# Gated linear attention into a two-layer MLP: attention output produced already transposed, with a reordered start and one more bank at the end

## The chip, the cores and the metric

The kernel runs on one core of a Trainium2 chip. The core has five engines that each run their own queue of instructions in order: TensorE (PE; matmuls, with weight loads listed as PEld), VectorE (DVE), ScalarE (ACT), GpSimd (POOL) and SyncE (SP, which here only issues DMAs). They meet through semaphores. Data lies in SBUF (128 partitions); matmuls write PSUM, which has eight banks. The metric is the device time of one execution in microseconds; the time of the kernel before is the median of 3 runs.

## The reference

The inputs q, k, v and f_logit are each (4, 8, 768, 48): batch B, heads H, time S, head dimension D. In float32:

```
f = 1 / (1 + exp(-f_logit))
for t in range(S):
    state = f[:, :, t, :, None] * state + einsum('bhd,bhde', k_t, v_t)
    y[:, :, t] = einsum('bhd,bhde->bhe', q_t, state)
x = y.transpose(0, 2, 1, 3).reshape(3072, 384)
h = x @ w_in            # 384 x 2048
out = maximum(0.01 * h, h) @ w_out   # 2048 x 384
```

The output is (3072, 384) float32.

## The kernel before

**Units.** Time is cut into chunks of 128 steps. A unit is one chunk of one batch entry with all 8 heads: 6 chunks x 4 batch entries = 24 units, numbered chunk by chunk, so that units 0 to 3 are the first chunk of each batch entry (c == 0) and units 20 to 23 the last. A state per batch entry is carried from chunk to chunk, in float32 (state_f) and bf16 (state_b); heads lie in pairs, two to a block of 128 columns, each head padded from 48 to 64.

**Attention of a unit.**
- load (L82): four DMAs on SP, f, k, q, v, 192 KB each, into pool inp with 6 buffers per name.
- gate_act (L106): ScalarE computes exp and log of f; gate_pe (L113): TensorE sums the logs over time with a triangular matrix ut, and the whole chunk's sum per column.
- decay_act (L124): ScalarE turns the sums into two factors, em and a, and the chunk's decay a_end.
- scale (L137): kh = k * em and qh = q * a. For units 0 and 1 kh is on VectorE; all else is on GpSimd.
- cast_v (L143): GpSimd copies v to bf16.
- turn_pe, turn_dve (L149, L156): TensorE transposes kh and qh in pairs of heads into one PSUM bank (ps_t); VectorE copies kT out, and copies q out in two 64-partition halves into qbd, a block-diagonal form whose other blocks are zero (cleared once, L75).
- score_pe (L165): four matmuls of kT against 256 columns of qbd; each gives the scores of two heads. Two banks (ps_w), each filled by two matmuls. mask_dve (L175): VectorE multiplies each bank by ut.
- mix_pe (L182): y, with time in the partitions and heads in the columns. For c > 0 eight matmuls of qbd with state_b (48 columns each), then eight of the masked scores with v (48 columns each).
- state_pe, state_dve, state_pool (L200, L211, L220): the new state, with the float32 update on VectorE and GpSimd and one bf16 copy on GpSimd. The last chunk skips these.
- y_act, x_pe, x_dve (L228, L233, L240): ScalarE copies y to bf16, TensorE transposes it in three blocks of 128 columns, VectorE copies the result out as xT, with the model dimension in the partitions.

**MLP of a unit.** up (L246) is called in four quarters: 12 matmuls of w_in against xT into one of two banks (ps_m), then a leaky ReLU on ScalarE into g. down (L258) is called in two halves of eight matmuls each (384 columns), which accumulate in the one bank of ps_o (pm2); the first half reads the first half of w_out, the second half the second. put (L265): VectorE copies pm2 to osb, SP writes it out.

**Weights.** load_w_in (L91) is called twice, each time for half of the 2048 columns and with three DMAs on the queue of GpSimd; load_w_out (L97) is called twice with one DMA each. They convert from float32 to bf16 on the way. GpSimd issues them in its own order: it works through what stands ahead of them first.

**Order.** Nothing is reordered: each engine runs its instructions as the program writes them. First come the loads of units 0 to 4 (LA = 5), then a start written out by hand (L278 to L324): attention of unit 0 with the w_in loads, gates of unit 1, the first two quarters of up of unit 0, the first w_out half, the other two quarters, then attention of unit 1 with the gates of unit 2 in it. The loop (L326) goes over i = 1 to 25: load unit i + 4; turn unit i + 1; half of up of unit i; scores and masks of i + 1; gate, decay and scale of i + 2; the other half of up; mix and state of i + 1; gate_act of i + 3; half of down of unit i - 2 (LAG = 2); the turn of x of i + 1; the other half of down, and put. PSUM is full: 2 banks for up, 1 for down, 1 for the turns, 2 for scores, 2 shared (ps_s, tag sm) by the gate sums, y, the new state and the turned x.

Of the kernel before, what the change touches and what calls it, by code (L numbers as in the profile page):

```python
# [9 lines left out]
FP32 = mybir.dt.float32  # L10
# [5 lines left out]
def kernel(  # L16
# [22 lines left out]
    NU = len(units)  # L39

    const = ctx.enter_context(tc.tile_pool(name="const", bufs=1))
    inp = ctx.enter_context(tc.tile_pool(name="inp", bufs=6))
    work = ctx.enter_context(tc.tile_pool(name="work", bufs=3))
    gpool = ctx.enter_context(tc.tile_pool(name="gpool", bufs=5))
    opool = ctx.enter_context(tc.tile_pool(name="opool", bufs=4))
# [22 lines left out]
    lfs = [const.tile([128, H, 64], BF16, name=f"lf{i}", tag=f"lf{i}") for i in range(3)]  # L68
    qhs = [const.tile([128, H, 64], BF16, name=f"qh{i}", tag=f"qh{i}") for i in range(3)]
    khs = [const.tile([128, H, 64], BF16, name=f"kh{i}", tag=f"kh{i}") for i in range(3)]  # L70
    qbds = [const.tile([128, P2, 2, 128], BF16, name=f"qbd{i}", tag=f"qbd{i}") for i in range(2)]
    state_f = [const.tile([128, P2, D], FP32, name=f"sf{b}", tag=f"sf{b}") for b in range(B)]
    state_b = [const.tile([128, P2, D], BF16, name=f"sb{b}", tag=f"sb{b}") for b in range(B)]
    for t in lfs + qhs + khs + qbds:
        nc.vector.memset(t, 0.0)  # L75
    for t in state_f:
        nc.vector.memset(t, 0.0)


    raw = {}  # L80

    def load(u):  # L82
        c, b = units[u]
        r = {}
        for name, src in (("f", f_logit), ("k", k), ("q", q), ("v", v)):
            t = inp.tile([128, H, D], FP32, name=f"{name}_raw", tag=f"{name}_raw")
            nc.sync.dma_start(out=t, in_=src[b, :, c * C:(c + 1) * C, :].rearrange("h t d -> t h d"))
            r[name] = t
        raw[u] = r

    def load_w_in(part, parts):  # L91
        w = FF // parts
        for kk in range(NK):
            nc.gpsimd.dma_start(out=w_in_b[:, kk, part * w:(part + 1) * w],  # L94
                                in_=moe_w_in[kk * 128:(kk + 1) * 128, part * w:(part + 1) * w])
# [7 lines left out]
    st = {}  # L103


    def gate_act(u):  # L106
        f = raw[u]["f"]
        e = work.tile([128, H, D], FP32, name="e_t", tag="e_t")
        nc.scalar.activation(e, f, AF.Exp, scale=-1.0)  # L109
        lf = lfs[u % 3]  # L110
        nc.scalar.activation(lf[:, :, 0:D], e, AF.Ln, bias=1.0)  # L111
# [31 lines left out]
    def cast_v(u):  # L143
        r = raw.pop(u)
        v_b = work.tile([128, H, D], BF16, name="v_b", tag="v_b")
        nc.gpsimd.tensor_copy(out=v_b, in_=r["v"])  # L146
        st[u]["v"] = v_b

    def turn_pe(u):  # L149
        tp = ps_t.tile([128, 2, P2, 128], BF16, name="tp", tag="tp")  # L150
        for i, src in enumerate((khs[u % 3], qhs[u % 3])):
            for p in range(P2):
                nc.tensor.transpose(tp[:, i, p, :], src[:, 2 * p:2 * p + 2, :], ident)  # L153
        st[u]["tp"] = tp

    def turn_dve(u):  # L156
        tp = st[u].pop("tp")
        kT = work.tile([128, P2, 128], BF16, name="kT", tag="kT")
        nc.vector.tensor_copy(out=kT, in_=tp[:, 0])  # L159
        qbd = qbds[u % 2]  # L160
        nc.vector.tensor_copy(out=qbd[0:64, :, 0, :], in_=tp[0:64, 1])
        nc.vector.tensor_copy(out=qbd[64:128, :, 1, :], in_=tp[64:128, 1])  # L162
        st[u]["kT"] = kT

    def score_pe(u):  # L165
        kT, qbd = st[u].pop("kT"), qbds[u % 2]
        st[u]["pw"] = []
        for g in range(2):
            pw = ps_w.tile([128, 4, 128], FP32, name="pw", tag="pw")
            for i in range(2):  # L170
                p = 2 * g + i
                nc.tensor.matmul(pw[:, 2 * i:2 * i + 2, :], kT[:, p, :], qbd[:, p, :, :], start=True, stop=True)  # L172
            st[u]["pw"].append(pw)

    def mask_dve(u):  # L175
        st[u]["wm"] = []
        for pw in st[u].pop("pw"):
            wm = work.tile([128, 4, 128], BF16, name="wm", tag="wm", bufs=6)
            nc.vector.tensor_mul(wm, pw, ut[:, None, :].to_broadcast([128, 4, 128]))  # L179
            st[u]["wm"].append(wm)  # L180

    def mix_pe(u):  # L182
        c, b = units[u]
        s = st[u]
        qbd, v_b, wms = qbds[u % 2], s["v"], s.pop("wm")
        py = ps_s.tile([128, 512], FP32, name="py", tag="sm")
        n = H if c == 0 else 2 * H
        i = 0
        if c > 0:
            for h in range(H):  # L190
                nc.tensor.matmul(py[:, h * D:(h + 1) * D], qbd[:, h // 2, h % 2, :], state_b[b][:, h // 2, :],  # L191
                                 start=(i == 0), stop=(i == n - 1))
                i += 1
        for h in range(H):
            nc.tensor.matmul(py[:, h * D:(h + 1) * D], wms[h // 4][:, h % 4, :], v_b[:, h, :],  # L195
                             start=(i == 0), stop=(i == n - 1))
            i += 1
        s["py"] = py

    def state_pe(u):  # L200
        c, b = units[u]
        if c == NCH - 1:
            return
        kh, v_b = khs[u % 3], st[u]["v"]
        pt = ps_s.tile([128, P2, 2 * D], FP32, name="pt", tag="sm")
        for p in range(P2):
            nc.tensor.matmul(pt[:, p, :], kh[:, 2 * p:2 * p + 2, :], v_b[:, 2 * p:2 * p + 2, :],  # L207
                             start=True, stop=True)
        st[u]["pt"] = pt
# [10 lines left out]
    def state_pool(u):  # L220
        c, b = units[u]
        if c == NCH - 1:
            return
        sf = state_f[b]
        nc.gpsimd.tensor_mul(sf, sf, st[u]["a_end"][:, :, None].to_broadcast([128, P2, D]))  # L225
        nc.gpsimd.tensor_copy(out=state_b[b], in_=sf)

    def y_act(u):  # L228
        xn = work.tile([128, KD], BF16, name="xn", tag="xn")
        nc.scalar.copy(out=xn, in_=st[u].pop("py")[:, 0:KD])  # L230
        st[u]["xn"] = xn

    def x_pe(u):  # L233
        xn = st[u].pop("xn")
        px = ps_s.tile([128, NK, 128], BF16, name="px", tag="sm")
        for kk in range(NK):
            nc.tensor.transpose(px[:, kk, :], xn[:, kk * 128:(kk + 1) * 128], ident)  # L237
        st[u]["px"] = px

    def x_dve(u):  # L240
        xT = work.tile([128, NK, 128], BF16, name="xT", tag="xT", bufs=6)
        nc.vector.tensor_copy(out=xT, in_=st[u].pop("px"))  # L242
        st[u]["xT"] = xT


# [12 lines left out]
    def down(u, half):  # L258
        s = st[u]
        if half == 0:  # L260
            s["pm2"] = ps_o.tile([128, KD], FP32, name="pm2", tag="pm2")
        for ff in range(8 * half, 8 * half + 8):
            nc.tensor.matmul(s["pm2"], s["g"][:, ff, :], w_out_b[:, ff, :], start=(ff == 0), stop=(ff == NF - 1))  # L263

# [5 lines left out]
        st.pop(u)  # L270


    LA = 5
    LAG = 2
    for u in range(LA):
        load(u)

    gate_act(0)  # L278
    gate_pe(0)
    decay_act(0)  # L280
    scale(0)
    load_w_in(0, 2)
    cast_v(0)
    load_w_in(1, 2)
    turn_pe(0)
    turn_dve(0)
    score_pe(0)
    mask_dve(0)
    mix_pe(0)
    y_act(0)  # L290
    x_pe(0)
    x_dve(0)
    state_pe(0)
    state_dve(0)
    state_pool(0)

    gate_act(1)
    gate_pe(1)
    decay_act(1)
    up(0, 0)  # L300
    up(0, 1)
    scale(1)
    cast_v(1)
    load_w_out(0, 2)
    up(0, 2)
    up(0, 3)
    turn_pe(1)
    turn_dve(1)
    gate_act(2)
    gate_pe(2)  # L310
    score_pe(1)
    mask_dve(1)
    decay_act(2)
    scale(2)
    cast_v(2)
    load_w_out(1, 2)
    mix_pe(1)
    y_act(1)
    x_pe(1)
    x_dve(1)  # L320
    state_pe(1)
    state_dve(1)
    state_pool(1)
    gate_act(3)  # L324

    for i in range(1, NU + LAG):  # L326
        n1, n2, n3, d = i + 1, i + 2, i + 3, i - LAG
        if i + LA - 1 < NU:
            load(i + LA - 1)
        if n1 < NU:  # L330
            turn_pe(n1)
            turn_dve(n1)
        if i < NU:
            up(i, 0)
            up(i, 1)
        if n1 < NU:
            score_pe(n1)
            mask_dve(n1)
        if n2 < NU:
            gate_pe(n2)  # L340
            decay_act(n2)
            scale(n2)
            cast_v(n2)
        if i < NU:
            up(i, 2)
            up(i, 3)
        if n1 < NU:
            mix_pe(n1)
            y_act(n1)
            state_pe(n1)  # L350
            state_dve(n1)
            state_pool(n1)
        if n3 < NU:
            gate_act(n3)
        if d >= 0:
            down(d, 0)
        if n1 < NU:
            x_pe(n1)
            x_dve(n1)
        if d >= 0:  # L360
            down(d, 1)
            put(d)

# [29 lines left out]
```

## Time and profile before

| | |
|---|---|
| median of 3 runs | 205.89 us (205.06 to 206.22) |
| the profiled execution | 205.08 us, of it a span of 203.3 us from first to last instruction |
| TensorE busy | 183.2 us, 90% of the span |
| ScalarE, VectorE, GpSimd busy | 109.2, 98.6, 75.3 us |
| share of TensorE in the chain that ended last | 85% (L254 up 32%, L263 down 31%) |
| share of DMA in that chain | 7% |
| moved by DMA | 25.17 MB read, 4.72 MB written |

How to read the lines below. A page line of an engine has its busy time, share of the span and count; the rows of digits give, for 40 equal slices of the span, the busy share in tenths. A line of the chain has start, length, engine, tile and line of the kernel. A timeline line has start, length, engine, line, operation, what is written <- what is read, shapes, count, and in brackets the idle time before it with what ended it. Matmuls are pipelined, so the recorded length of a group is longer than the distance from its start to the next group's start. q0 is the DMA queue that GpSimd issues to, q1 that of SP.

### The profile page before, as it was taken

What the parts mean: (1) busy time and instruction counts of PE and PEld (TensorE: products, weight loads), DVE (VectorE), ACT (ScalarE), POOL (GpSimd) and SP (SyncE); (2) the same over time, 40 slices, a digit from 0 to 9 for tenths busy, and PEclk for the clock granted to TensorE, in tenths of its full rate; (3) what the DMA queues carried; (4) which work ended last, traced back from release to release, by engine and by line L of the source; (5) the groups of instructions that cost most, each with busy time, mean ns of one, the idle gap of its engine ahead of it and who ended that gap; (6) DMA issues with size and microseconds to landing.
All of it is one profiled execution on the core that took longest, in us unless ns stands there. A gap on an engine that the chain in (4) does not pass through costs nothing.

```text
span 203.3 us, 5831 instructions
## 1 busy us (share of the span) xinstructions
PE 183.2 (90%) x2432; PEld 149.2 (73%) x2432; DVE 98.6 (48%) x225; ACT 109.2 (54%) x237; POOL 75.3 (37%) x127
## 2 busy tenths in 40 slices
PE   0446778999999999999999999999999999999973
PEld 0224658977887887897788788789779878877741
DVE  8450155654664565455465456445546534533021
ACT  4142446856844854764674584485467458533400
POOL 2743064536415514623641651562363244120000
PEclk9999999999999999999999999999999999999999
DMA  6999999999976946865874785595585671110111
GB/s 132 189 158 203 191 200 179 186 191 201 215 144 116 193 95 128 172 136 106 152 165 97 128 173 116 109 194 126 111 155 118 141 135 42 40 41 2 42 54 62
DMA packets 106267, 27.12 MB, mean 133 GB/s; under 512 B 100352, under 2 KB 105472, under 8 KB 106240
## 3 DMA queue, kind: packets, MB, share of 16 engines
q1 hardware_dynamic: 103296, 23.60, 59.7%
q0 software_dynamic: 2944, 3.15, 9.4%
q8 instruction: 19, 0.31, 0.7%
q14 instruction: 8, 0.07, 0.1%
HBM read 25.17 MB, written 4.72 MB: 147 GB/s over the span
## 4 chain that ended last, share of the span: by engine, by line
PE 85%; DMA 7%; ACT 3%; POOL 2%; DVE 1%; issue 1%
PE pm L254 32%; PE pm L263 31%; PE pw L172 6%; DMA w_in_b<-in_moe_w_in_dram 5%; PE tp L153 5%; PE py L195 2%; PE px L237 2%; PE cs L117 2%; PE py L191 2%; PE pt L207 2%; DMA f_raw<-in_f_logit_dram 1%; POOL w_in_b L94 1%; DVE osb L268 1%; PE cs L120 1%; DVE wm L179 1%
## 5 line engine op out<-in xcount | busy, mean ns | idle before, releaser
L256 ACT ACTIVATE gT<-pm 128x512 bf16<-128x512 f32 x96 | 56.2, 601 | 63.0 <-PE pm L254 61.3
L254 PE MATMUL pm<-xT,w_in_b 128*128 128x128 bf16 x1152 | 76.0, 224 | 3.9 <-DMA w_in_b<-in_moe_w_in_dram 3.9
L254 PEld LDWEIGHTS <-w_in_b 128*128 128x128 bf16 x1152 | 69.2, 101 | 5.4 <-DMA w_in_b<-in_moe_w_in_dram 4.7
L263 PE MATMUL pm<-w_out_b,gT 128*128 128x384 bf16 x384 | 69.7, 326 | 1.3 <-DVE osb L268 1.3
L140 POOL TENSOR_TENSOR kh<-k_raw,em_t 128x384 bf16<-128x384 f32 x22 | 20.1, 915 | 93.0 <-ACT em_t L129 88.2
L263 PEld LDWEIGHTS <-gT 128*128 128x128 bf16 x384 | 35.4, 98 | 20.9 <-issue 1.8
L179 DVE TENSOR_TENSOR wm<-pw,ut 128x512 bf16<-128x512 f32 x48 | 30.9, 687 | 12.6 <-PE pw L172 12.6
L268 DVE COPY osb<-pm 128x384 f32<-128x384 f32 x24 | 13.4, 558 | 30.4 <-PE pm L263 30.4
L141 POOL TENSOR_TENSOR qh<-q_raw,a_t 128x384 bf16<-128x384 f32 x24 | 21.9, 914 | 4.6 <-ACT a_end L133 4.5
L242 DVE COPY xT<-px 128x384 bf16<-128x384 bf16 x24 | 8.6, 358 | 23.6 <-PE px L237 23.6
L217 DVE TENSOR_TENSOR sf<-sf,pt 64x192 f32<-64x192 f32 x20 | 6.9, 346 | 20.9 <-PE pt L207 19.3
L172 PE MATMUL pw<-qbd,kT 128*128 128x256 bf16 x96 | 15.2, 282 | 1.3 <-DVE qbd L162 1.3
L159 DVE COPY kT<-tp 128x512 bf16<-128x512 bf16 x24 | 10.0, 417 | 11.2 <-PE tp L153 11.0
L109 ACT ACTIVATE e_t<-f_raw 128x384 f32<-128x384 f32 x24 | 12.8, 533 | 4.8 <-DMA f_raw<-in_f_logit_dram 4.8
L129 ACT ACTIVATE em_t<-cs 128x384 bf16<-128x384 f32 x24 | 11.8, 491 | 6.1 <-PE cs L120 5.2
L230 ACT CAST xn<-py 128x384 bf16<-128x384 f32 x24 | 11.4, 473 | 6.6 <-PE py L195 6.6
L117 PE MATMUL cs<-lf,ut 128*128 128x384 bf16 x24 | 8.3, 345 | 5.8 <-ACT lf L111 5.8
L111 ACT ACTIVATE lf<-e_t 128x384 bf16<-128x384 f32 x24 | 12.6, 523 | 0.8
L172 PEld LDWEIGHTS <-kT 128*128 128x128 bf16 x96 | 9.4, 99 | 4.2 <-DVE kT L159 0.8
L146 POOL CAST v_b<-v_raw 128x384 bf16<-128x384 f32 x24 | 12.1, 504 | 0.6 <-DMA v_raw<-in_v_dram 0.6
L130 ACT ACTIVATE a_t<-cs 128x384 bf16<-128x384 f32 x24 | 11.6, 484 | 0.0
L225 POOL TENSOR_TENSOR sf<-sf,a_end 128x192 f32<-128x192 f32 x20 | 10.1, 505 | 3.7 <-DVE sf L218 3.7
(38 smaller groups left out, 153.5 us busy)
## 6 DMA issues: line engine op xcount, KB each, us to landing
f_raw<-in_f_logit_dram SPq DMA_DIRECT2D x24, 192.0 KB, 3.1
k_raw<-in_k_dram SPq DMA_DIRECT2D x24, 192.0 KB, 4.4
q_raw<-in_q_dram SPq DMA_DIRECT2D x24, 192.0 KB, 4.2
v_raw<-in_v_dram SPq DMA_DIRECT2D x24, 192.0 KB, 4.3
out_dram<-osb SPq DMA_DIRECT2D x24, 192.0 KB, 2.0
w_in_b<-in_moe_w_in_dram POOLq DMA_DIRECT2D x6, 256.0 KB, 8.4
w_out_b<-in_moe_w_out_dram POOLq DMA_DIRECT2D x2, 768.0 KB, 9.7
```

The costliest lines, as they stand in the source:

```text
L109: nc.scalar.activation(e, f, AF.Exp, scale=-1.0)
L111: nc.scalar.activation(lf[:, :, 0:D], e, AF.Ln, bias=1.0)
L117: nc.tensor.matmul(cs[:, 0:H * D], ut, lf[:, :, 0:D], start=True, stop=True)
L140: eng.tensor_mul(khs[u % 3][:, :, 0:D], r["k"], st[u]["em"])
L141: nc.gpsimd.tensor_mul(qhs[u % 3][:, :, 0:D], r["q"], st[u]["a"])
L146: nc.gpsimd.tensor_copy(out=v_b, in_=r["v"])
L172: nc.tensor.matmul(pw[:, 2 * i:2 * i + 2, :], kT[:, p, :], qbd[:, p, :, :], start=True, stop=True)
L179: nc.vector.tensor_mul(wm, pw, ut[:, None, :].to_broadcast([128, 4, 128]))
L254: nc.tensor.matmul(pm[:, i, :], w_in_b[:, kk, ff * 128:(ff + 1) * 128], s["xT"][:, kk, :], start=(kk == 0), stop=(kk == NK - 1))
L256: nc.scalar.activation(s["g"][:, 4 * g:4 * g + 4, :], pm, AF.Prelu, alpha=0.01)
L263: nc.tensor.matmul(s["pm2"], s["g"][:, ff, :], w_out_b[:, ff, :], start=(ff == 0), stop=(ff == NF - 1))
L268: nc.vector.tensor_copy(out=osb, in_=st[u]["pm2"])
```

## The change

- **x comes out transposed.** mix_pe now writes y with the model dimension in the partitions, straight into a tile py of [128, 3, 128], and y_act, x_pe and x_dve give way to one VectorE copy from PSUM, y_dve. The 384 rows of the result are cut into 12 groups of 32; group g lies in block g // 4 at partitions 32 * (g % 4). A pair of heads has three groups: 32 columns of the first head, 16 of each, 32 of the second. For c > 0 each group takes one matmul with 32 columns of state_b as weights and the pair's qT (128 columns) as moving data. For the masked scores each pair takes four: the outer groups from v_b, and the middle group twice from v2, a copy of v's middle 32 columns spread to 64 with 16 zero columns beside each half.
- **Scores without the block-diagonal q.** turn_dve copies q out whole as qT. score_pe takes eight matmuls of 48 partitions and 128 columns, one per head, the first heads of the pairs into one bank and the second heads into the other, alternating.
- **What this brings along.** qbd goes; v2 (three tiles, cleared once, filled by GpSimd in cast_v) comes. state_b becomes block-diagonal, twice as wide, cleared once, and GpSimd fills it by two copies of 64 partitions.
- **The start.** Only units 0 and 1 are loaded at first. A DMA of two elements on SP, hold, reads from the third piece of w_in's first half, so SP waits until that piece has landed; then it issues unit 2, and units 3 to 5 behind it. The pool inp has 7 buffers. The order of units 0 to 2 is new: half of up of unit 0, attention of unit 1, half of up of unit 1, gates of unit 2, w_out, the rest of up of unit 0, and attention of unit 2 with the rest of up of unit 1 and the gates of unit 3 between its parts. The loop begins at i = 2.
- **Two last banks.** The last even unit's down (unit 22) accumulates in the bank of the turns, not in that of ps_o.

```diff
-    inp = ctx.enter_context(tc.tile_pool(name="inp", bufs=6))
+    inp = ctx.enter_context(tc.tile_pool(name="inp", bufs=7))
...
-    qbds = [const.tile([128, P2, 2, 128], BF16, name=f"qbd{i}", tag=f"qbd{i}") for i in range(2)]
+    v2s = [const.tile([128, P2, 4, 16], BF16, name=f"v2{i}", tag=f"v2{i}") for i in range(3)]
...
-    state_b = [const.tile([128, P2, D], BF16, name=f"sb{b}", tag=f"sb{b}") for b in range(B)]
-    for t in lfs + qhs + khs + qbds:
+    state_b = [const.tile([128, P2, 2 * D], BF16, name=f"sb{b}", tag=f"sb{b}") for b in range(B)]
+    for t in lfs + qhs + khs + v2s + state_b:
         nc.vector.memset(t, 0.0)
...
+    hold = const.tile([1, 2], BF16, tag="hold")
...
+        v2 = v2s[u % 3]
+        nc.gpsimd.tensor_copy(
+            out=v2[:, :, 0:4:3, :],
+            in_=r["v"].rearrange("t (p j) d -> t p (j d)", j=2)[:, :, 32:64].rearrange("t p (j e) -> t p j e", j=2))
...
-        qbd = qbds[u % 2]
-        nc.vector.tensor_copy(out=qbd[0:64, :, 0, :], in_=tp[0:64, 1])
-        nc.vector.tensor_copy(out=qbd[64:128, :, 1, :], in_=tp[64:128, 1])
+        qT = work.tile([128, P2, 128], BF16, name="qT", tag="qT")
+        nc.vector.tensor_copy(out=qT, in_=tp[:, 1])
...
-        for g in range(2):
-            pw = ps_w.tile([128, 4, 128], FP32, name="pw", tag="pw")
-            for i in range(2):
-                p = 2 * g + i
-                nc.tensor.matmul(pw[:, 2 * i:2 * i + 2, :], kT[:, p, :], qbd[:, p, :, :], start=True, stop=True)
+        pws = [ps_w.tile([128, P2, 128], FP32, name="pw", tag="pw") for j in range(2)]
+        for p in range(P2):
+            for j in range(2):
+                rows = slice(64 * j, 64 * j + D)
+                nc.tensor.matmul(pws[j][:, p, :], kT[rows, p, :], qT[rows, p, :], start=True, stop=True)
...
+    NQ = 3 * P2
...
+        py = ps_s.tile([128, NK, 128], FP32, name="py", tag="sm")
+        jobs = []
         if c > 0:
+            for g in range(NQ):
+                p, i = divmod(g, 3)
+                jobs.append((g, state_b[b][:, p, 32 * i:32 * i + 32], qT[:, p, :]))
+        for j in range(2):
+            for p in range(P2):
+                jobs.append((3 * p + 2 * j, v_b[:, 2 * p + j, 16 * j:16 * j + 32], wms[j][:, p, :]))
+            for p in range(P2):
+                jobs.append((3 * p + 1, v2[:, p, 2 * j:2 * j + 2, :], wms[j][:, p, :]))
+        left = [sum(1 for g, _, _ in jobs if g % 4 == r) for r in range(4)]
+        begun = [False] * 4
+        for g, lhsT, rhs in jobs:
+            kk, r = divmod(g, 4)
+            left[r] -= 1
+            nc.tensor.matmul(py[32 * r:32 * r + 32, kk, :], lhsT, rhs, start=not begun[r], stop=left[r] == 0)
+            begun[r] = True
...
-        nc.gpsimd.tensor_copy(out=state_b[b], in_=sf)
+        for j in range(2):
+            rows = slice(64 * j, 64 * j + 64)
+            nc.gpsimd.tensor_copy(out=state_b[b][rows, :, j * D:j * D + D], in_=sf[rows])
-    def y_act(u):
...
-    def x_pe(u):
...
-    def x_dve(u):
+    def y_dve(u):
         xT = work.tile([128, NK, 128], BF16, name="xT", tag="xT", bufs=6)
-        nc.vector.tensor_copy(out=xT, in_=st[u].pop("px"))
+        nc.vector.tensor_copy(out=xT, in_=st[u].pop("py"))
...
-            s["pm2"] = ps_o.tile([128, KD], FP32, name="pm2", tag="pm2")
+            pool, tag = (ps_t, "tp") if u >= NU - 2 and u % 2 == 0 else (ps_o, "pm2")
+            s["pm2"] = pool.tile([128, KD], FP32, name="pm2", tag=tag)
```

The start and the loop after the change; attend(u) is turn, scores, masks, mix, y_dve and state of one unit, one after another:

```
    LA = 4
    load(0)
    load(1)
    gate_act(0)
    gate_pe(0)
    decay_act(0)
    scale(0)
    load_w_in(0, 2)
    nc.sync.dma_start(out=hold, in_=w_in_b[0:1, NK - 1, 0:2])
    cast_v(0)
    load_w_in(1, 2)
    load(2)
    attend(0)
    gate_act(1)
    gate_pe(1)
    decay_act(1)
    scale(1)
    cast_v(1)
    up(0, 0)
    up(0, 1)
    attend(1)
    up(1, 0)
    up(1, 1)
    gate_act(2)
    gate_pe(2)
    decay_act(2)
    scale(2)
    load_w_out(0, 2)
    cast_v(2)
    load_w_out(1, 2)
    load(3)
    load(4)
    load(5)
    up(0, 2)
    up(0, 3)
    turn_pe(2)
    turn_dve(2)
    up(1, 2)
    score_pe(2)
    mask_dve(2)
    gate_act(3)
    gate_pe(3)
    decay_act(3)
    scale(3)
    cast_v(3)
    up(1, 3)
    mix_pe(2)
    y_dve(2)
    state_pe(2)
    state_dve(2)
    state_pool(2)
    gate_act(4)

    for i in range(2, NU + LAG):
...
        if n1 < NU:
            mix_pe(n1)
            y_dve(n1)
...
        if d >= 0:
            down(d, 0)
            down(d, 1)
            put(d)
```

More of the change, by code (lines that the diff above doesn't have):

```diff
@@ L146, in cast_v @@
         nc.gpsimd.tensor_copy(out=v_b, in_=r["v"])
-        st[u]["v"] = v_b
+        v2 = v2s[u % 3]
+        nc.gpsimd.tensor_copy(
+            out=v2[:, :, 0:4:3, :],
+            in_=r["v"].rearrange("t (p j) d -> t p (j d)", j=2)[:, :, 32:64].rearrange("t p (j e) -> t p j e", j=2))
+        st[u]["v"], st[u]["v2"] = v_b, v2
     def turn_pe(u):
@@ L159, in turn_dve @@
         nc.vector.tensor_copy(out=kT, in_=tp[:, 0])
-        qbd = qbds[u % 2]
-        nc.vector.tensor_copy(out=qbd[0:64, :, 0, :], in_=tp[0:64, 1])
-        nc.vector.tensor_copy(out=qbd[64:128, :, 1, :], in_=tp[64:128, 1])
-        st[u]["kT"] = kT
+        qT = work.tile([128, P2, 128], BF16, name="qT", tag="qT")
+        nc.vector.tensor_copy(out=qT, in_=tp[:, 1])
+        st[u]["kT"], st[u]["qT"] = kT, qT
     def score_pe(u):
-        kT, qbd = st[u].pop("kT"), qbds[u % 2]
-        st[u]["pw"] = []
-        for g in range(2):
-            pw = ps_w.tile([128, 4, 128], FP32, name="pw", tag="pw")
-            for i in range(2):
-                p = 2 * g + i
-                nc.tensor.matmul(pw[:, 2 * i:2 * i + 2, :], kT[:, p, :], qbd[:, p, :, :], start=True, stop=True)
-            st[u]["pw"].append(pw)
+        kT, qT = st[u].pop("kT"), st[u]["qT"]
+        pws = [ps_w.tile([128, P2, 128], FP32, name="pw", tag="pw") for j in range(2)]
[3 more added lines that the diff above has]
+                nc.tensor.matmul(pws[j][:, p, :], kT[rows, p, :], qT[rows, p, :], start=True, stop=True)
+        st[u]["pw"] = pws
     def mask_dve(u):
@@ L177, in mask_dve @@
         for pw in st[u].pop("pw"):
-            wm = work.tile([128, 4, 128], BF16, name="wm", tag="wm", bufs=6)
-            nc.vector.tensor_mul(wm, pw, ut[:, None, :].to_broadcast([128, 4, 128]))
+            wm = work.tile([128, P2, 128], BF16, name="wm", tag="wm", bufs=6)
+            nc.vector.tensor_mul(wm, pw, ut[:, None, :].to_broadcast([128, P2, 128]))
             st[u]["wm"].append(wm)
+    NQ = 3 * P2
     def mix_pe(u):
@@ L184, in mix_pe @@
         s = st[u]
[L185 to L188, printed above, removed]
+        qT, v_b, v2, wms = s.pop("qT"), s["v"], s.pop("v2"), s.pop("wm")
+        py = ps_s.tile([128, NK, 128], FP32, name="py", tag="sm")
+        jobs = []
         if c > 0:
[L190 to L197, printed above, removed]
+            for g in range(NQ):
[13 more added lines that the diff above has]
+            begun[r] = True
         s["py"] = py
@@ L225, in state_pool @@
         nc.gpsimd.tensor_mul(sf, sf, st[u]["a_end"][:, :, None].to_broadcast([128, P2, D]))
-        nc.gpsimd.tensor_copy(out=state_b[b], in_=sf)
-    def y_act(u):
-        xn = work.tile([128, KD], BF16, name="xn", tag="xn")
-        nc.scalar.copy(out=xn, in_=st[u].pop("py")[:, 0:KD])
-        st[u]["xn"] = xn
-    def x_pe(u):
[L234 to L238, printed above, removed]
-    def x_dve(u):
+        for j in range(2):
+            rows = slice(64 * j, 64 * j + 64)
+            nc.gpsimd.tensor_copy(out=state_b[b][rows, :, j * D:j * D + D], in_=sf[rows])
+    def y_dve(u):
         xT = work.tile([128, NK, 128], BF16, name="xT", tag="xT", bufs=6)
-        nc.vector.tensor_copy(out=xT, in_=st[u].pop("px"))
+        nc.vector.tensor_copy(out=xT, in_=st[u].pop("py"))
         st[u]["xT"] = xT
@@ L270, in put, with attend @@
         st.pop(u)
-    LA = 5
+    LA = 4
     LAG = 2
-    for u in range(LA):
-        load(u)
+    def attend(u):
+        turn_pe(u)
+        turn_dve(u)
+        score_pe(u)
+        mask_dve(u)
+        mix_pe(u)
+        y_dve(u)
+        state_pe(u)
+        state_dve(u)
+        state_pool(u)
+    load(0)
+    load(1)
     gate_act(0)
@@ L282 @@
     load_w_in(0, 2)
+    nc.sync.dma_start(out=hold, in_=w_in_b[0:1, NK - 1, 0:2])
     cast_v(0)
     load_w_in(1, 2)
[L285 to L295, printed above, removed]
+    load(2)
+    attend(0)
     gate_act(1)
@@ L299 @@
     decay_act(1)
+    scale(1)
+    cast_v(1)
     up(0, 0)
     up(0, 1)
-    scale(1)
-    cast_v(1)
-    load_w_out(0, 2)
+    attend(1)
+    up(1, 0)
+    up(1, 1)
+    gate_act(2)
+    gate_pe(2)
+    decay_act(2)
+    scale(2)
+    load_w_out(0, 2)
+    cast_v(2)
+    load_w_out(1, 2)
+    load(3)
+    load(4)
+    load(5)
     up(0, 2)
     up(0, 3)
[L307 to L323, printed above, removed]
-    gate_act(3)
-    for i in range(1, NU + LAG):
+    turn_pe(2)
[3 more added lines that the diff above has]
+    mask_dve(2)
+    gate_act(3)
+    gate_pe(3)
[10 more added lines that the diff above has]
+    for i in range(2, NU + LAG):
         n1, n2, n3, d = i + 1, i + 2, i + 3, i - LAG
-        if i + LA - 1 < NU:
-            load(i + LA - 1)
+        if i + LA < NU:
+            load(i + LA)
         if n1 < NU:
@@ L348 @@
             mix_pe(n1)
-            y_act(n1)
+            y_dve(n1)
             state_pe(n1)
@@ L356 @@
             down(d, 0)
[L357 to L360, printed above, removed]
             down(d, 1)
```

## The prediction

> **What bounds the kernel now.** I read the page's busy rows first, then the chain that ended last, then the timeline of one iteration, then the start and the end. From the page:
>
> ```profile
> PE 183.2 (90%) x2432; PEld 149.2 (73%) x2432; DVE 98.6 (48%) x225; ACT 109.2 (54%) x237; POOL 75.3 (37%) x127
> PE   0446778999999999999999999999999999999973
> DMA  6999999999976946865874785595585671110111
> ```
>
> TensorE is full from the eighth slice (about 36 us) on; before that it has holes while the DMA engines are full. So there are two regimes, a start of some 36 us and a dense loop, and a short tail. One iteration in the chain (start, us, what):
>
> ```profile
> 94.09 0.45 PE tp L153 x8
> 94.54 1.34 PE pm L254 x24
> 95.88 0.57 PE pw L172 x4
> 96.69 1.36 PE pm L254 x24
> 98.25 0.20 PE py L195 x8
> 98.63 1.30 PE pm L263 x8
> 100.09 1.30 PE pm L263 x8
> 101.39 0.45 PE tp L153 x8
> ```
>
> It is TensorE alone, 101.39 - 94.09 = 7.30 us per unit: no other engine appears. The timeline of the same iteration gives the pieces to be replaced:
>
> ```profile
> 95.38 0.43 DVE L162 COPY qbd<-tp 64x512 bf16<-64x512 bf16 x1
> 95.86 0.60 PE L172 MATMUL pw<-qbd,kT 128*128 128x256 bf16 x4
> 97.89 0.36 PE L191 MATMUL py<-sb,qbd 128*128 128x48 bf16 x8
> 98.09 0.36 PE L195 MATMUL py<-v_b,wm 128*128 128x48 bf16 x8
> 98.30 0.33 PE L207 MATMUL pt<-v_b,kh 128*128 128x96 bf16 x4
> ```
>
> Recorded lengths contain a latency, so I go from start to start. Up's first half starts at 94.38 and takes 24 x 56 ns, to 95.72; the scores start at 95.86, when the third VectorE copy ends: a stall of 0.14. Scores 0.43 (95.86 to 96.29, when the gate starts). Mix 97.89 to 98.30 = 0.41, or 16 pairs of weight load and matmul at 25.6 ns each. The three turns of x (L237) start at 99.76, the next layer's half at 99.93: 0.17. Together 0.14 + 0.43 + 0.41 + 0.17 = 1.15 us of the 7.30. A 128-column matmul is 56 ns, a 384-column one 162.5 ns (1.30 / 8).
>
> **The loop after the change.** Out go the stall (two copies of about 0.4 us instead of three end 0.4 us earlier), four 256-column scores, sixteen mix matmuls and three turns. In come eight scores of 128 columns on 48 rows each, and in mix 12 matmuls from the state and 16 from the masks, each with 32 weight columns and 128 moving columns. The trace has no matmul on a part of the array. Bounds: serial at 56 ns, 36 x 56 = 2.02 us. From below, two scores abreast and four mix matmuls abreast, 4 x 56 + 7 x 56 = 0.62 us. Between stands the pair rate of the old mix, the fastest that any weight load with matmul goes in this trace: 36 x 25.6 = 0.92 us. I take it, since it is the row nearest in kind (many small matmuls, each with its own weights). Then an iteration changes by 0.92 - 1.15 = -0.23 us; with 20 full iterations (units 4 to 23 attended in the loop) -4.6 us. The ends give 20 x -0.53 = -10.6 and 20 x +0.87 = +17.4. A switch between whole and part array is also unseen; there are four per iteration. From below zero, from above one matmul's latency beyond its spacing, 0.219 - 0.056 = 0.16 us, so 0 to 0.65 us per iteration; I take zero, as the trace's changes between 128-, 48- and 384-column matmuls show no gap, but keep +13 us as the other end.
>
> A rule to weigh: the Trainium skill, "TensorEngine Tiling (Array Packing)", section Key Properties, says that a change of tiling mode drains TensorE, which speaks against this change, without a figure. "TensorE: Matmul & The Clock Gate", Part 3, gives about 4 ns per further tile of a pack and none of this case's rows shows it; by that, an estimate, scores and mix would take 4 x 60 + 7 x 68 = 0.72 us, and the loop would change by 20 x -0.43 = -8.6 us in place of my -4.6.
>
> Beside TensorE and hidden: ScalarE loses a 0.47 us copy per unit, but has 61.3 us of waits for L254 alone, no gain. VectorE swaps 0.41 + 0.43 + 0.36 (two half copies, xT from bf16) for 0.41 + 0.56 (qT; xT from f32, as the osb copy), 0.23 less. GpSimd gains a copy of v2 (128 elements; the 192- and 384-element casts take 0.36 and 0.50, so about 0.3) and a second state copy, 0.36. It waits 4.15 us for em_t in this iteration, and the turn needs qh only 2 us after it is ready, so 0.66 is covered; uncovered it would be 20 x 0.66 = 13 us. Both score banks now fill together, so the masks (1.29 us) begin only at the end of the scores; gate and up's second half (0.26 + 1.34) lie over them, then the state's twelve matmuls. In set-up, VectorE drops 1.0 us of qbd and clears v2 and state_b, about 1.4 by the 192- and 256-word memsets; it was idle 0.69 us before kh, which covers the 0.4.
>
> **The start.** Rows for it (timeline, then DMA of 10 to 20 us, then issue to landing of w_out):
>
> ```profile
> 16.67 2.63 PE L254 MATMUL pm<-xT,w_in_b 128*128 128x128 bf16 x23 [1.22 <-DMA w_in_b<-in_moe_w_in_dram]
> q0 software_dynamic: 844, 1.53, 87.4%
> q1 hardware_dynamic: 1402, 0.27, 19.7%
> 28.80 0.94 POOL L99 DMA_DIRECT2D w_out_b<-in_moe_w_out_dram  x1
> DMA to landing us min/median/max: 9.0/9.7/10.3
> ```
>
> 23 matmuls in 2.63 us are 107 ns apart, though the granted clock reads 1.00 there; 56 ns comes only after about 31 us. I cost the start at 107. The weights' queue (q0) already takes 85% of the bytes while it runs, so holding unit 2 back, behind SP's wait on the third piece of w_in, can give it at most the rest: 16.67 becomes about 16.3. SP's held loads 2 to 5 are not missed: after w_in's second half (20.95) each 192 KB takes 1.0 us at 200 GB/s, f of unit 2 lands at 21.3, unit 2 whole at 24.3, f of unit 3 at 25.3.
>
> What costs is the order on ScalarE and GpSimd. Up of unit 0, half: 16.3 + 2.5 = 18.8. Attention of unit 1, by the old one's gaps: turn to copies 1.09, two copies 0.8, scores to masks 0.63, masks 1.29, mix 0.4, xT 0.56 + 0.2: x at 23.8. Half of up of unit 1: 26.4. gate_act(2) stands behind that unit's last leaky ReLU on ScalarE: 0.65, then 1.1 for exp and log: gate 28.2. decay 0.6, em to kh 0.6, kh and qh 0.9 each on GpSimd: 31.2. Meanwhile TensorE does the rest of up of unit 0, to 31.3. Only now w_out's first half is issued, 31.3 against 16.30 before. Turn 0.6, half of up 0.9, ReLU, exp, log 1.9: gate of unit 3 at 34.7; its qh at 37.5, and TensorE turns it then, against 35.92: +1.6. The first down half would follow at 41.7 (before 40.05), the second at 43.0 (41.52). But w_out's second half queues behind the first: 31.3 + 2.9 (the pause between w_in's issue at 7.21 and q0's first bytes at 10.1) + 2 x 0.786 MB at 140 to 180 KB/us (first half between 20.95 and 26.6; w_in) = 43 to 45.5. I take 45: the second down half starts at 45 against 41.52, **+3.5 us**. Bounds: 0 if TensorE already runs at 56 ns from 24 us (2 x 1.2 us less, and the weights issued as much sooner), +5.5 if w_out lands at 9.0 + 5.7 from 31.3, 46, and the scores go one by one.
>
> **The tail.**
>
> ```profile
> 196.56 0.56 DVE L268 COPY osb<-pm 128x384 f32<-128x384 f32 x1 [2.85 <-PE pm L263]
> 197.18 2.76 PE L263 MATMUL pm<-w_out_b,gT 128*128 128x384 bf16 x16 [0.65 <-DVE osb L268]
> ```
>
> The last three downs start at 190.35, 193.77, 197.18, 3.41 apart, for 16 x 162.5 ns = 2.60 of work. With unit 22 in the freed turn bank each follows at once: 2 x 0.81 = **-1.6 us**. After it the same copy and output remain.
>
> **Sum.** -4.6 + 3.5 - 1.6 = -2.7 us. On the profiled execution, 205.08 us (span 203.3 and 1.8 around it), 202.4; on the median of 205.89, 203.2. The profiled run lies low among three of 205.06 to 206.22, so I take the middle, 202.8.
>
> **Rivals.**
> - *Four abreast.* The parts of the array work side by side: 0.62 us in place of 0.92, 20 x 0.30 = 6.0 less: 196.8. For it: turn, layer and mix already go without gaps, so the sequencer keeps up at 25.6 ns with two instructions each. Against: no row shows less.
> - *One after another (slower).* Part-array matmuls share one stream: 36 x 56 = 2.02, iteration +0.87, 202.8 + 4.6 + 17.4 = 224.8. The change loses as soon as 20 x D + 1.9 > 0, D = -0.095, or 1.055 us for 36: **29 ns per matmul**, only 15% above my row. For it: nothing in the trace runs abreast. Against: weights load under a running matmul everywhere here.
> - *Switches.* Pair rate holds but four changes cost 0.05 to 0.16 each: +4 to +13, 206.8 to 215.8.
> - *The early reorder costs nothing.* TensorE is at 56 ns sooner and w_out never late: 199.3, the rest as forecast.
>
> **How the numbers follow.** Likeliest case, pair rate and a late w_out: 0.40, own range 200 to 205.5. Four abreast, or no loss at the start: 0.25, 194 to 200. Switches or 29 to 40 ns: 0.22, 205.5 to 213. One by one: 0.13, 213 to 230. The range 196 to 212 leaves out about 0.13 above, 0.02 of the switches and 0.05 below. A measurement here can tell about 0.5% from no change, 204.9 to 206.9: same gets 0.08 (the edges of the first and third case); faster 0.25 + 0.34 = 0.59; slower 0.33.
>
> **What would show it.** Loop: iterations near 7.07 us, eight scores starting some 0.2 us before the gate, 28 mix matmuls in about 0.72; 0.4 would be the first rival, 1.6 the second, gaps at the four changes the third. Start: gate of unit 2 waiting on ScalarE near 26 to 28 us, w_out issued near 31, a wait of TensorE for w_out_b near 43 to 45, which is absent in before. Tail: no wait for osb. I am wrong if part-array matmuls are far from 25.6 ns, or if TensorE's 107 ns ends early.

## The result, and the profile after

The changed kernel takes 208.09 us (median of 4 runs, 207.78 to 208.45) against 205.71 us before: 1.0118 times as long, 95% interval 1.0083 to 1.0153. It is slower by 2.4 us. The profiled executions take 207.78 and 205.08 us, with spans of 205.7 and 203.3. Some executions of a kernel take over 1.5% longer than its fastest; the medians and ratios below leave those out. The time lies inside the range that I gave, but on the other side of before than the forecast.

From the page of after, the rows of slices of TensorE and of the granted clock:

```profile
PE   1446757939999999999999999999999999999992
PEclk9999796996999999999999999999999999999999
```

The ninth slice (41 to 46 us), 9 before, now has a 3: TensorE was full by then and falls idle again. The slice after it shows a clock of 6. The chain that ended last names the wait, and then shows one dense iteration (start, us, what):

```profile
31.87 13.39 DMA w_out_b<-in_moe_w_out_dram
45.30 1.57 PE pm L266 x8
46.88 0.85 PE tp L159 x8
47.73 2.45 PE pm L256 x24
...
55.60 0.45 PE tp L159 x8
56.05 1.34 PE pm L256 x24
57.39 0.33 PE pw L176 x8
57.72 0.27 PE cs L119
57.99 0.08 PE cs L122 x4
58.07 1.36 PE pm L256 x24
59.43 0.51 PE py L208 x28
59.93 0.28 PE pt L219 x4
60.21 2.60 PE pm L266 x16
62.81 0.45 PE tp L159 x8
```

The second half of w_out, issued at 31.87, lands at 45.3, and the first layer's second down half, which began at 41.52 before, begins at 45.30. Behind the wait eight downs take 1.57 us from the first start to the last end (1.46 at full pace), the two turns 0.85 instead of 0.45, half of up 2.45 instead of 1.34: 1.6 us lost before full pace returns. The granted clock of the windows fell in that time, to 0.66 (us, PE busy, then the other engines, PEclk, DMA share, GB/s):

```profile
40.00:45.00 5.00, 1.88 (x28) 1.10 (x25) 1.17 (x3) 1.54 (x4) 2.90 (x7) 1.00 1.25 197
45.00:50.00 5.00, 4.70 (x40) 4.10 (x39) 1.31 (x3) 0.60 (x1) 0.00 (x0) 0.66 0.61 140
```

An iteration is 62.81 - 55.60 = 7.21 us, 0.09 less than before. Its timeline, another iteration, the matmuls around scores and mix:

```profile
99.13 1.50 PE L256 MATMUL pm<-xT,w_in_b 128*128 128x128 bf16 x24
100.56 0.40 PE L176 MATMUL pw<-qT,kT 48*128 48x128 bf16 x8
100.89 0.34 PE L119 MATMUL cs<-lf,ut 128*128 128x384 bf16 x1
102.60 0.35 PE L208 MATMUL py<-qT,sb 128*32 128x128 bf16 x12
102.94 0.23 PE L208 MATMUL py<-wm,v 128*32 128x128 bf16 x4
103.11 0.34 PE L219 MATMUL pt<-v_b,kh 128*128 128x96 bf16 x4
```

Twenty-four matmuls from 99.13 at 56 ns end at 100.47, yet the scores start at 100.56. Eight scores two abreast would take 0.22, and the gate starts 0.33 behind their start. The mix's twelve state matmuls take 0.18 (102.60 to 102.78, where the next group starts), 15 ns each; its last four, from 102.94, would be through by 103.00 four abreast, but the state's matmul starts at 103.11. So the matmuls of the mix are as fast as the lower bound of the prediction, and so are the scores if 0.11 of their 0.33 us belongs to the change behind them; about 0.1 us is lost around each change between whole and part array.

The tail, one group of 48 downs without a wait:

```profile
193.88 7.96 PE L266 MATMUL pm<-w_out_b,gT 128*128 128x384 bf16 x48
```

The account by landmarks of the two traces: second down half 45.30 - 41.52 = +3.8; slow stretch +1.6; 20 iterations x -0.09 = -1.8; tail 2 x -0.81 = -1.6; from the last copy's start to the end of the span 3.8 us (201.88 to 205.7) instead of 3.3 (199.97 to 203.3), +0.5. Together +2.5; the spans differ by 2.4.

### The profile page after: what moved, and what is told of

The parts are those of the page before. It is cut to its first block, busy times and chain, and to the rows that moved or that the text cites. A ratio compares the mean times of both kernels' runs of the same rounds, so it can differ in the third digit from the quotient of the medians.

```text
span 205.7 us, 6487 instructions
## 1 busy us (share of the span) xinstructions
PE 181.0 (88%) x2728; PEld 141.7 (69%) x2728; DVE 91.9 (45%) x206; ACT 99.8 (49%) x213; POOL 88.0 (43%) x171
## 4 chain that ended last, share of the span: by engine, by line
PE 79%; DMA 12%; POOL 3%; issue 2%; DVE 2%; ACT 1%; POOLq 0%
PE pm L256 30%; PE pm L266 30%; DMA w_out_b<-in_moe_w_out_dram 7%; PE py L208 5%; PE tp L159 5%; DMA w_in_b<-in_moe_w_in_dram 4%; PE pw L176 3%; PE cs L119 3%; PE pt L219 2%; DMA f_raw<-in_f_logit_dram 1%; DVE wm L183 1%; PE cs L122 1%; POOL w_in_b L96 1%; POOL qh L143 1%; POOL w_out_b L101 0%
## 5 line engine op out<-in xcount | busy, mean ns | idle before, releaser
L256 PE MATMUL pm<-xT,w_in_b 128*128 128x128 bf16 x1152 | 76.9, 225 | 3.8 <-DMA w_in_b<-in_moe_w_in_dram 3.4
L266 PE MATMUL pm<-w_out_b,gT 128*128 128x384 bf16 x384 | 66.3, 326 | 3.4 <-DMA w_out_b<-in_moe_w_out_dram 3.4
L266 PEld LDWEIGHTS <-gT 128*128 128x128 bf16 x384 | 36.3, 98 | 26.0 <-issue 3.6
L244 DVE CAST xT<-py 128x384 bf16<-128x384 f32 x24 | 13.4, 558 | 22.2 <-PE py L208 22.2
L240 POOL CAST sb<-sf 64x192 bf16<-64x192 f32 x40 | 14.0, 350 | 2.5
L237 POOL TENSOR_TENSOR sf<-sf,a_end 128x192 f32<-128x192 f32 x20 | 10.1, 507 | 10.5 <-DVE sf L230 9.4
L159 PE MATMUL tp<-ident,kh 128*128 128x128 bf16 x96 | 10.2, 234 | 1.4 <-DVE kh L142 1.2
L176 PE MATMUL pw<-qT,kT 48*128 48x128 bf16 x192 | 9.8, 222 | 1.9 <-DVE qT L167 1.9
L159 PEld LDWEIGHTS <-kh 128*128 128x128 bf16 x96 | 7.8, 105 | 4.4 <-DVE kh L142 1.3
```

Source lines behind the costliest of these rows:

```text
L176: nc.tensor.matmul(pws[j][:, p, :], kT[rows, p, :], qT[rows, p, :], start=True, stop=True)
L240: nc.gpsimd.tensor_copy(out=state_b[b][rows, :, j * D:j * D + D], in_=sf[rows])
L244: nc.vector.tensor_copy(out=xT, in_=st[u].pop("py"))
L256: nc.tensor.matmul(pm[:, i, :], w_in_b[:, kk, ff * 128:(ff + 1) * 128], s["xT"][:, kk, :], start=(kk == 0), stop=(kk == NK - 1))
```

## The experiments

The theory after the traces (A): the new start issues w_out too late and loses more than loop and tail give; the loop gives little since four changes of the array per iteration cost 0.1 us each. The rivals: the loss sits in the loop (B); the loads bound the start whatever the order (D).

**One part alone.** The first kernel, called loop_only, has the new attention and the two last banks with the old start (scores and mix of the diff, order, five first loads and 6 buffers of before):

```diff
-    LA = 4
+    LA = 5
...
-    for i in range(2, NU + LAG):
+    for i in range(1, NU + LAG):
```

> The start, the loads and the 6 buffers of before, with the new attention (scores by head, x in 32-column groups) and the two last banks of after. My reading of the two traces (theory A): the loop gains only 0.09 us per unit (7.21 against 7.30 us), since four changes between whole and part array take back 0.4 us of the 0.5 that four-abreast matmuls save; the two banks gain 1.6 us; the loss of after comes from its new start. Then this kernel is faster than before: -1.9 - 1.6 = -3.5 us, or -3 to -5 (some ScalarE and TensorE steps of the start go too). Rival B: the loss of after is in the loop itself (part-array matmuls slow somewhere, or GpSimd's longer work late): then it is slower than before by 1 to 3 us. Rival C: the early part of the loop profits from the pair rate of my forecast: -4.6 - 1.6 = -6.2 us.

Measured: 201.91 us against 205.69 us, ratio 0.9825 (0.9782 to 0.9869), 3.8 us faster. In its chain the iteration has the length of after's, and there is no wait for w_out:

```profile
39.88 2.60 PE pm L265 x16
42.48 0.45 PE tp L158 x8
...
49.69 0.45 PE tp L158 x8
```

7.21 us per iteration. The downs begin at 39.72 by the timeline, 0.3 ahead of before. B falls, and so does C.

The second, start_only, has the new start with the old attention and one last bank.

> The start, the hold and the 7 buffers of after, with the old attention (block-diagonal q, x turned by TensorE) and one bank for down. Theory A: w_out is issued near 31 us, TensorE waits for its second half until near 45 us (against 41.5 in before), and then runs its next 2 us at half pace: slower than before by 4 to 6 us. Rival B (the loss of after lies in the loop): within 1 us of before.

Measured: 213.26 us, ratio 1.0364 (1.0326 to 1.0402), 7.6 us slower, more than the 4 to 6 expected. From its timeline:

```profile
33.02 0.96 POOL L101 DMA_DIRECT2D w_out_b<-in_moe_w_out_dram  x1
43.96 1.46 PE L265 MATMUL pm<-w_out_b,gT 128*128 128x384 bf16 x8
47.93 2.71 PE L265 MATMUL pm<-w_out_b,gT 128*128 128x384 bf16 x8 [2.34 <-DMA w_out_b<-in_moe_w_out_dram]
```

With the longer old attention w_out is issued 2.8 us later still than in after (30.22), the second down half is 6.4 us behind before, and the slow stretch behind it costs 1.6 more. But only part of the 6.4 is the wait of A (2.34 us): the first down half, ahead of that wait, already starts 3.9 us behind before (43.96 against 40.05; 40.42 in after). With the old attention the new order is late even where no w_out is missing. The new start loses with either attention.

**The late w_out.** wout_early is after with one edit:

```diff
+    load_w_out(0, 2)
+    load_w_out(1, 2)
     gate_act(2)
     gate_pe(2)
     decay_act(2)
     scale(2)
-    load_w_out(0, 2)
     cast_v(2)
-    load_w_out(1, 2)
```

> After with one edit: both halves of w_out are issued by GpSimd before the scaling of unit 2 instead of behind it, near 25 us instead of 30.2 and 31.9. Theory A: w_out's second half lands near 39 us, TensorE's wait of 3.4 us and the slow 2 us behind it (1.8 us lost) go: 5.2 us less than after, near 202.9, so 2.8 us faster than before. Rival D: w_out then takes the DMA engines from units 3 and 4, whose k and q come late, and TensorE waits for these instead: within 1.5 us of after.

Measured: 203.58 us, ratio 0.989 (0.985 to 0.993): 4.5 us less than after, and faster than before. Its timeline:

```profile
26.09 1.85 POOL L101 DMA_DIRECT2D w_out_b<-in_moe_w_out_dram  x2
28.19 0.48 PE L119 MATMUL cs<-lf,ut 128*128 128x384 bf16 x1 [1.65 <-ACT lf L113]
34.16 0.32 PE L119 MATMUL cs<-lf,ut 128*128 128x384 bf16 x1 [1.07 <-ACT lf L113]
41.24 2.76 PE L266 MATMUL pm<-w_out_b,gT 128*128 128x384 bf16 x16
```

Sixteen downs in 2.76 us: no wait, and no slow stretch behind it. The second down half comes 2.8 us earlier than in after, and the 1.6 of the slow stretch go: 4.4 of the 4.5. (The 1.8 of the expectation sets the first eight downs against 1.30, a distance between starts, and not against their recorded 1.46.) Moving two instructions on GpSimd's queue by 4 to 5 us is worth 4.5 us, so the late w_out with the slow stretch that follows is what made after slower than before. D falls here. The rest of the new start's handicap to loop_only (1.7 us) lies ahead of the first downs, which start at 41.24 against 39.72. TensorE waits 1.65 and 1.07 us for the logs there, because ScalarE works through leaky ReLUs first; how much of the 1.7 these two waits make is not shown.

**The hold.** no_hold is wout_early without the DMA that SP waits for.

```diff
-    nc.sync.dma_start(out=hold, in_=w_in_b[0:1, NK - 1, 0:2])
```

> wout_early without the hold: SP issues unit 2, and units 3 to 5 behind it, at once. Theory A (w_in's queue already takes 85% of the bytes while it runs, and 16.2 against 16.7 us for the third piece of w_in is all that the hold gave): 0.2 to 0.6 us slower than wout_early (203.6), not to be told from no change. Rival B (unit 2's loads hold w_in up): 1 to 3 us slower. Rival C (the hold only delays unit 2): up to 1 us faster.

Measured: 203.24 us (0.9909 of before, 0.9871 to 0.9947), not to be told from wout_early. The group of up that follows the third piece of w_in starts at 17.36 us, against 17.16 in wout_early; but it starts at 16.21 in after, which is the same program up to there, so a single trace can't size the hold. B falls; between A and C the runs can't decide, and either way the hold is worth no more than about 1 us.

**The tail.** one_bank is after with unit 22's down in the one bank:

```diff
-            pool, tag = (ps_t, "tp") if u >= NU - 2 and u % 2 == 0 else (ps_o, "pm2")
+            pool, tag = ps_o, "pm2"
```

> After with unit 22's down in the one bank of ps_o, as in before. If the two last banks are worth what the gaps of before say, it is 1.6 us slower than after (near 209.7); if something else sets the end (the last output, for one), it is within 0.5 us of after.

Measured: 210.43 us, 2.3 us slower than after. The timeline has the gaps of before again:

```profile
195.41 2.76 PE L266 MATMUL pm<-w_out_b,gT 128*128 128x384 bf16 x16
198.83 2.76 PE L266 MATMUL pm<-w_out_b,gT 128*128 128x384 bf16 x16 [0.65 <-DVE osb L271]
202.24 2.76 PE L266 MATMUL pm<-w_out_b,gT 128*128 128x384 bf16 x16 [0.65 <-DVE osb L271]
```

3.42 and 3.41 us apart instead of 2.60: 1.6 us. In its trace what is over lies in the start: here the wait for w_out ended at 45.80, not 45.30, and the slow stretch was longer (eight downs in 2.72 us instead of 1.57). Its length differs from run to run.

**What makes the small matmuls fast.** mix_by_group adds one line to loop_only:

```diff
+        jobs.sort(key=lambda job: job[0] % 4)
```

> The kernel with the old start and the new loop (loop_only), with one line more: mix's 28 matmuls are sorted by column group, so that seven in a row go to the same 32 columns instead of four in a row to four different ones. Theory A (the new mix is fast because neighbours in the order run side by side in different column groups): each matmul then takes its 56 ns alone, 28 x 56 = 1.57 us instead of 0.40, an iteration is 8.4 us instead of 7.21, and the kernel some 23 us slower than loop_only. Rival B (a matmul with 32 weight columns is simply cheap, 15 to 20 ns, wherever it goes): no change, within 1 us.

Measured: 212.45 us, 10.5 us slower than loop_only; the iteration is 7.75 us, 0.54 more. Neither expectation fits in size. Some of its mix, from the timeline (from qT: state matmuls, from wm: mask matmuls of the group before):

```profile
108.76 0.34 PE L208 MATMUL py<-qT,sb 128*32 128x128 bf16 x3
108.94 0.22 PE L208 MATMUL py<-wm,v_b 128*32 128x128 bf16 x1
108.95 0.23 PE L208 MATMUL py<-qT,sb 128*32 128x128 bf16 x1
109.00 0.22 PE L208 MATMUL py<-wm,v 128*32 128x128 bf16 x1
109.02 0.22 PE L208 MATMUL py<-qT,sb 128*32 128x128 bf16 x1
109.05 0.22 PE L208 MATMUL py<-wm,v_b 128*32 128x128 bf16 x1
```

Within one column group the matmuls start 50 to 70 ns apart, as A says: B falls. But the second group's first state matmul (108.95) starts while three of the first group's seven are still to start: about two groups run at once, and 28 matmuls take 0.96 us (108.76 to the last one's 109.66 and its 0.06), not 1.57. So what makes them fast is that neighbours in the order go to different column groups; sorting them badly costs half a microsecond per iteration.

**The changes of the array.** split_mix puts the state's twelve matmuls between the last two quarters of up, the same work with two more changes per iteration:

```diff
             up(i, 2)
+            if n1 < NU:
+                mix_state(n1)
             up(i, 3)
```

> loop_only with mix cut in two: the twelve matmuls from the state go between the third and the fourth quarter of up, the sixteen from the masks stay. The work is the same, but the array changes from whole to part and back once more in each iteration. Theory A (each change between whole and part array costs about 0.1 us, the gaps seen around scores and mix): 0.2 us more per iteration, 20 iterations: 4 us slower than loop_only (201.9). Rival B (the gaps are waits for masks, for qT or for a bank): no change, within 0.8 us.

Measured: 207.31 us, ratio 1.0082 to before, 5.4 us more than loop_only. The chain:

```profile
103.28 0.45 PE tp L158 x8
...
105.75 0.69 PE pm L268 x12
106.44 0.28 PE py L197 x12
106.72 0.78 PE pm L268 x12
107.50 0.34 PE py L220 x16
...
110.71 0.45 PE tp L158 x8
```

7.43 us, 0.22 more than 7.21: 0.11 for each change. Twenty times that is 4.4; the other 1.4 us of its profiled run lie ahead of the loop (first downs at 41.24 in the chain, against 39.88), behind a late f; the edit adds nothing to TensorE's work there, since the first chunk has no state matmuls.

whole_scores gives the eight scores all 128 partitions (so each is the sum of two heads) and takes two changes out:

```diff
-                rows = slice(64 * j, 64 * j + D)
+                rows = slice(0, 128)
```

> loop_only with the eight score matmuls on all 128 partitions instead of 48, so that each gives the sum of the two heads of its pair and not the one head's scores: the array is then whole from the turn to the mix. Theory A: pairs no longer run side by side, 8 x 56 = 0.45 us, but the gaps before and behind the scores (0.09 and 0.11 us) go: the iteration stays at 7.21 within 0.05 us and the time within 1 us of loop_only. Rival B (pairs side by side are worth 0.2 us and the gaps belong to something else): 0.2 us more per iteration, 4 to 5 us slower.

Measured: 201.75 us (ratio 0.9811, 0.9764 to 0.9858), the time of loop_only, with 7.22 us per iteration (turns at 100.41 and 107.63):

```profile
102.20 0.45 PE pw L175 x8
102.64 0.16 PE cs L118
```

Scores and gate sum are 0.61 us here and 0.33 + 0.27 = 0.60 in after's chain. Running pairs of scores side by side saves 0.22 us and the two changes that it needs take it all back.

three_changes runs the attention one unit further ahead from iteration 6 on, so that the scores of one unit and the mix of the unit before meet, and the gate sums stand between the last two quarters of up:

```diff
+        if n2 < NU:
+            score_pe(n2)
         if n1 < NU:
             mix_pe(n1)
             y_dve(n1)
+        if n2 < NU:
+            mask_dve(n2)
```

> loop_only with the attention in the loop run one unit further ahead from iteration 6 on, so that the scores of one unit and the mix of the unit before stand next to each other: TensorE changes between whole and part array three times per iteration instead of four; the work is the same. Theory A (a change costs about 0.1 us): 7.10 us per iteration instead of 7.21, 17 iterations, 1.5 to 2 us less than loop_only (201.9), up to 1 us of it lost where the order changes. Rival B (the gaps are waits for masks or copies, which now have a whole iteration): all four gaps go, 0.4 us per iteration, 6 to 7 us less. Rival C (the change from rows to columns costs as much as two): no gain.

Measured: 200.46 us, ratio 0.9736 (0.9693 to 0.978), 1.5 us less than loop_only:

```profile
101.98 0.45 PE tp L158 x8
...
103.77 0.33 PE pw L175 x8
104.10 0.50 PE py L207 x28
...
109.08 0.45 PE tp L158 x8
```

7.10 us: one change fewer, 0.11 us less, so the change from rows to columns costs as much as one and not two (C). Adding two, taking out two and taking out one all give 0.11 us for a change. That the other gaps stay with masks that have a whole iteration's time excludes waits for masks; as for copies, qT is there 0.46 us before the scores start in after (100.10 against 100.56). B falls. What the array does in these 0.11 us no run shows. This is a version that beats both kernels.

**The start once more.** early_gates moves the gates of units 2 and 3 ahead of ScalarE's leaky ReLUs and issues w_out behind the scaling of unit 2:

```diff
     turn_dve(1)
+    gate_act(2)
     score_pe(1)
     mask_dve(1)
+    gate_pe(2)
+    decay_act(2)
+    scale(2)
+    cast_v(2)
+    load_w_out(0, 2)
+    load_w_out(1, 2)
...
     mix_pe(1)
```

> After with its start written again: exp, log and gate of unit 2 go into the attention of unit 1 (between its scores and its mix), those of unit 3 behind the first leaky ReLU of unit 1, and w_out is issued as soon as unit 2 is scaled, near 24 us. Theory A (what delays after is the order on ScalarE and GpSimd and, behind it, the late w_out): TensorE's waits for the gates of units 2 and 3 (1.65 and 1.07 us), for qh of unit 3 (0.5) and for w_out (3.4) go, and the slow stretch behind the last; the loop begins near 32 to 33 us instead of 36, the time is 198 to 201. Rival D (the loads bound the start: unit 3 or w_out can't be there sooner): not below 203.

Measured: 202.13 us (201.59 to 204.23), ratio 0.9835 (0.977 to 0.99): 1.4 us under wout_early, but the two intervals overlap. It lies between the 198 to 201 of A and the 203 of D. The loop began at 32.7 us, but w_out was issued at 26.09, as in wout_early, and not near 24. In the view of TensorE's waits (from whom, us in total, times, longest):

```profile
PE cs L119 <- ACT lf L113: 5.9, 2, 4.8
PE pm L266 <- DMA w_out_b<-in_moe_w_out_dram: 1.3, 1, 1.3
PE pm L256 <- ACT gT L258: 1.2, 1, 1.2
```

The wait for the log of unit 3 went. That of unit 2 is still 1.15 us (the 5.9 less the first unit's 4.8), now because ScalarE itself waits 1.69 us for unit 2's f. The last wait is for a leaky ReLU that stands on ScalarE behind the exp of unit 4, whose f landed only at 33.5. The DMA engines are full at that time (share 1.27 from 30 to 40 us, 184 and 191 GB/s). So with the order mended all three waits stand behind loads, as D has it, though A's gain came in part; whether another order of the loads would shorten them was not tried.

The last, both, is this start with the loop of three_changes.

> The start of early_gates with the loop of three_changes. If the two gains are independent, 1 to 2 us less than early_gates; if the tighter start leaves the loads of units 5 to 8 late for the loop that runs one unit further ahead, no less.

Measured: 200.32 us, ratio 0.9741 (0.9684 to 0.9798), 1.8 us less than early_gates and the time of three_changes. The gain of the loop is there. The start adds nothing to it, as it had nothing to add: early_gates (202.13) only comes to the time of loop_only, which has the old start (201.91).

## Why the prediction failed, point by point

- **The loop, -4.6 forecast, -1.8 measured: the step that failed.** It is the term for switches of the array, which I set to zero since changes between 128-, 48- and 384-column matmuls show no gap in the trace of before. Those are all on the whole array, so they told nothing. Measured: 0.11 us per change, four per iteration, 0.44 us, inside the 0 to 0.65 that I had as bounds. The matmuls themselves were faster than the pair rate that I took: 0.62 us for 36, the lower bound (8 / 2 x 56 + 28 / 4 x 56 ns): 0.40 for the mix, and 0.22 for the scores, their 0.33 less a change. So two of my rivals, four abreast and switches, happened together: 0.62 + 0.44 = 1.06 against 1.15, the 0.09 of the chain. That the loop came out 2.8 us off and not more is luck: the pair rate was 6.0 us too dear over 20 iterations, the zero for switches 8.8 too cheap.
- **The weighed rule.** The Trainium skill, "TensorEngine Tiling (Array Packing)", section Key Properties, says that changing the tiling mode drains TensorE. The runs fit that and give the cost a size, 0.11 us here. The estimate by "TensorE: Matmul & The Clock Gate", Part 3 (0.72 us for scores and mix, a sum of -8.6) was near the 0.62 measured for the matmuls, but had only the half that favours the change.
- **The start, +3.5 forecast, +3.8 measured.** The mechanism was right: gate of unit 2 at 27.44 behind ScalarE (28.2 forecast), w_out issued at 30.22 (31.3), second half landed at 45.3 (45), 158 KB/us between the two halves' landings. One step in between was off: unit 3 was turned at 36.12 and not at 37.5, since TensorE was at full pace at 27.7 already. It made only the wait longer.
- **A term that was missing: +1.6 us.** Behind the wait of 3.4 us TensorE fell back to about half pace for the next 2 us of work. I had read the slow pace in the early part of before and did not ask whether a new wait would bring it back.
- **The tail, -1.6 forecast, -1.6 in the trace.** Right.
- **What was held to be hidden** (ScalarE, VectorE, GpSimd's extra copies) was hidden: no wait of TensorE for any of them stands in the dense loop.
- **The sum.** With the loop at its measured -1.8 the sum is 3.5 - 1.8 - 1.6 = +0.1, no change; with 1.6 for the slow stretch as well it is +1.7. It took both to turn the forecast's sign.

## What to carry to other kernels

Matmuls on a part of the array pay for the way in and out: here 0.11 us per change, so put the part-array work of one iteration together, and order it so that neighbours go to different parts. When a start is reordered, follow each weight load to the instruction that it stands behind on its issuing engine; two DMA issues moved by 4 to 5 us were worth 4.5 us. A wait of TensorE costs more than its length when the clock falls behind it: here 1.6 us on top of 3.4.

## What the runs showed of the hardware that was not expected

- In a mix sorted by column group, matmuls of the next group start about 0.19 us after the group before them, with three of its seven still to start: recorded starts do not follow the program's order across column groups, and with four groups in turn twelve matmuls start in 0.18 us.
- The slow stretch after a wait for w_out has no fixed length: eight downs behind it took 1.57 us in after, 2.72 in one_bank and 2.71 in start_only, against 1.46 at full pace. In early_gates, behind a wait of 1.27 us, they took 1.46: there was no slow stretch.
